# Windowed attention and a feed-forward layer on one core: the order of the instructions set by a list schedule inside the kernel

## The chip, the cores and the metric

One core of a Trainium2 chip runs the kernel alone. The metric is the device time of one execution in microseconds (us), lower is better; a kernel is given by the median of its runs. The core's engines each work through a queue of their own in order: TensorE (PE: matmuls, and PEld: its weight loads), VectorE (DVE), ScalarE (ACT), GpSimd (POOL) and SyncE (SP), whose queue issues the transfers here. An instruction that waits for another engine holds up everything behind it on its own engine.

## The reference

Attention over 8 batches, 8 heads, 576 positions and 64 values a head, with a causal window of 128 and a bias that falls with the distance; its output, as 4608 tokens of 512 values, goes through a feed-forward layer of 2048 hidden units with a piecewise quadratic gate.

```python
scores = scale * np.matmul(q, k.transpose(0, 1, 3, 2))
bias = slopes[:, None, None] * (-np.abs(rel).astype(np.float32))[None, :, :]
mask = (rel >= 0) & (rel < window)
scores = np.where(mask, scores + bias[None], -1000000000.0)
scores = scores - np.max(scores, axis=-1, keepdims=True)
attn = np.exp(scores)
attn = attn / (np.sum(attn, axis=-1, keepdims=True) + 1e-09)
x = np.matmul(attn, v)
...
h = x @ w_in
g = np.where(pos, h, np.where(neg, 0.0, (h + beta) ** 2 / (4.0 * beta)))
return (g @ w_out).astype(np.float32)
```

The inputs q, k and v are float32; the two weight matrices come as 64-bit floats and are turned into 32-bit ones in the kernel.

## The kernel before

The 4608 tokens are cut into ten chunks (`SIZES`): the first and the last have 256 tokens, the eight between them 512. A chunk goes through attention head by head and then through a sweep of the feed-forward layer over eight groups of hidden units. The attention of chunk c+1 is woven into the sweep of chunk c, so that TensorE has both kinds of work.

**Attention of a head m** (steps `scores`, `weights_t`, `values`). TensorE multiplies queries and keys for two blocks of 128 queries at a time into one PSUM bank (`s`); VectorE picks the older or newer key of each place and adds the distance (L304, L306, result `z`, with the maximum `nmax`); ScalarE takes the exponential with the sum (L308); VectorE makes the reciprocal `rc` (L310, L311); the weights are scaled (L316 on ScalarE, four instructions of one block; L313 on VectorE in the first three chunks); TensorE turns them over (`p`, L324); ScalarE and VectorE split them into a rounded high part and a rest (`lu`, L340, L341); GpSimd masks both parts with two instructions over 1024 columns (L348, L350); TensorE multiplies with the values (`x`, L379), and ScalarE and VectorE put the result into `xn` (L384, L385). Before that, ScalarE and VectorE split keys (`kk`, `kl`: L261, L262, one instruction each over both heads of a pair), queries (`ql`: L250, L251) and values (`vs`: L271, L272). In the first three chunks (`LIGHT`) the matmuls are plain float32 ones without a split.

**A sweep** (`sweep_steps`). For each of the eight groups g of a 512-token chunk, seven products after Strassen's scheme (`PRODUCTS`, six matmuls of 256 columns each, L427) replace the eight of the plain one. They use two PSUM banks in turn, `hA` and `hB`. After products 0, 2 and 4 (weights A11, S2, S1) ScalarE copies `hA` out into `s0`, `s2`, `s4` (L561); after product 5 (S4) it copies `hA` into `h0` (L567); VectorE adds `hB` and such a copy after products 1, 4 and 6 (L563, L565, L569). A bank takes its next product only after that. Then the gate (`nonlinear`): clamp on VectorE (L434, `m`), square on ScalarE (L435), maximum on VectorE (L440), rounded copy `gh` on ScalarE (L447), rest `gl` on VectorE (L448). The second layer (`layer2`) then takes three matmuls of 512 columns for each of 16 hidden blocks and four token tiles (L462, L463, L464); each finished tile is copied out as `o` (L467) and stored.

The inputs of a sweep are seven combinations of quarters of `xn`, split again into two parts (`split_x`, `combine`; `x_T1`, `x_B11` and so on). The combinations of weights are made once in the sweep of chunk 1 (`build`), written to device memory, and fetched again for each later chunk (`fetch`, L182) into a ring of ten buffers, one fetch for each product used. All transfers go through the one SP queue.

**What sets the order.** The program is written in the order in which the loops at the end call the steps, and the framework's scheduler then places the instructions of each engine after a model of their times; a few stretches are raised or lowered by hand (`high_priority` with `URGENT` for the copies and adds that free a bank, `issue_after` for the conversion of weights). The framework places single matmuls, so those of a product or of a layer-2 tile can be parted.

Of the kernel before, what the change touches and what calls it, by code (L numbers as in the profile page):

```python
# [8 lines left out]
F32 = mybir.dt.float32  # L9
# [23 lines left out]

@with_exitstack
def windowed_attention_then_ffn(
# [29 lines left out]
    const = ctx.enter_context(tc.tile_pool(name="const", bufs=1))  # L65
    wp = ctx.enter_context(tc.tile_pool(name="wp", bufs=NFC + 1))
    ring = ctx.enter_context(tc.tile_pool(name="ring", bufs=10))
    xp = ctx.enter_context(tc.tile_pool(name="xp", bufs=1))
    fp = ctx.enter_context(tc.tile_pool(name="fp", bufs=2))
    ap = ctx.enter_context(tc.tile_pool(name="ap", bufs=1))  # L70
    dr = ctx.enter_context(tc.tile_pool(name="dr", bufs=1, space=DRAM))
    ps_acc = ctx.enter_context(tc.tile_pool(name="ps_acc", bufs=2, space=PSUM))
    ps_h = ctx.enter_context(tc.tile_pool(name="ps_h", bufs=1, space=PSUM))
    ps_a = ctx.enter_context(tc.tile_pool(name="ps_a", bufs=2, space=PSUM))

    turn = [0]

    def bank(c, name):
        turn[0] += 1
        if c < FIRST and turn[0] % 2:  # L80
            return ps_acc.tile([P, 4 * P], F32, name=name, tag="acc1")
        return ps_a.tile([P, 4 * P], F32, name=name, tag="ps_a")
# [15 lines left out]
    dist = ap.tile([P, P], I32, name="dist", tag="qr")  # L98
# [3 lines left out]
    t = ap.tile([P, 2, P], F32, name="t", tag="kr")  # L102
    V.tensor_copy(t[:, 0], dist)
    V.tensor_scalar(t[:, 1], t[:, 0], float(-P), None, ALU.add)
    V.tensor_scalar(older, t[:, 0], 0.0, None, ALU.is_gt)
    V.copy_predicated(t[:, 0], older, t[:, 1])
    V.tensor_copy(rel[:, 0], t[:, 0])
    G.affine_select(out=rel[:, 1], in_=t[:, 0], pattern=[[-1, P]], base=0, channel_multiplier=1,
                    compare_op=ALU.is_ge, fill=NEG)
    V.tensor_copy(rel[:, 2], t[:, 0])  # L110
    V.tensor_copy(rel[D:, 2], rel[D:, 1])
    V.memset(rel[D:, 2, :D], NEG)
    V.tensor_copy(rel[:, 3], t[:, 0])
# [7 lines left out]
    w_of = {}  # L121
    raw = {}
# [5 lines left out]
    def fetch_raw(i):  # L128
        fc, n = WEIGHTS[i]
        r = raw[i] = xp.tile([P, DM, 2], I32, name=f"raw_{i}", tag=RAW_IN[i % len(RAW_IN)])  # L130
        DMA.dma_start(r.rearrange("p f w -> p (f w)"), (wo32 if n else wi32)[fc])

    def convert(i):
        fc, n = WEIGHTS[i]
        r = raw.pop(i)
        low, high = r[..., 0], r[..., 1]
        if fc not in w_of:
            w_of[fc] = wp.tile([P, 2, DM], F32, name=f"w{fc}", tag="w")
# [575 lines left out]
```

## Time and profile before

| what | us |
|---|---|
| median of 3 runs | 1096.57 |
| lowest and highest of them | 1090.62, 1100.12 |
| the profiled execution | 1102.9 |
| its span, first to last instruction | 1101.2 |

The profile is of one execution. "Busy" of an engine is the time in which at least one of its instructions was running. Matmuls overlap one another, and their ends are modelled, so the rate of TensorE is read from the times between starts. The granted clock of TensorE is given as a share of its full clock. In the answers that list waits, the first name waited for the second; in those that list windows, each engine has its busy time and in brackets how many instructions.

### The profile page before, as it was taken

What the parts mean: (1) busy time and instruction counts of PE and PEld (TensorE: products, weight loads), DVE (VectorE), ACT (ScalarE), POOL (GpSimd) and SP (SyncE); (2) the same over time, 40 slices, a digit from 0 to 9 for tenths busy, and PEclk for the clock granted to TensorE, in tenths of its full rate; (3) what the DMA queues carried; (4) which work ended last, traced back from release to release, by engine and by line L of the source; (5) the groups of instructions that cost most, each with busy time, mean ns of one, the idle gap of its engine ahead of it and who ended that gap; (6) DMA issues with size and microseconds to landing.
All of it is one profiled execution on the core that took longest, in us unless ns stands there. A gap on an engine that the chain in (4) does not pass through costs nothing.

```text
span 1101.2 us, 19641 instructions
## 1 busy us (share of the span) xinstructions
PE 1037.2 (94%) x6432; PEld 914.3 (83%) x6432; DVE 810.6 (74%) x2058; ACT 724.4 (66%) x1850; POOL 202.2 (18%) x226
## 2 busy tenths in 40 slices
PE   7899899998999999998989899989999999999998
PEld 6677688897888788887878788978887888889897
DVE  6888788887667887586768777687758766875453
ACT  6987577666667777566757676667756766764342
POOL 2311333311102021021111211112102111221000
PEclk8999999999999999998999999999989999999999
DMA  9683554556555666556656566565655655665562
GB/s 320 199 280 114 176 177 164 182 186 193 179 170 170 196 189 182 153 162 196 177 147 187 177 185 184 156 207 162 181 155 175 206 156 168 176 204 163 152 220 67
DMA packets 101909, 198.04 MB, mean 180 GB/s; under 512 B 11312, under 2 KB 14896, under 8 KB 101808
## 3 DMA queue, kind: packets, MB, share of 16 engines
q1 hardware_dynamic: 101808, 196.78, 58.3%
q8 instruction: 52, 0.85, 0.3%
q14 instruction: 49, 0.40, 0.1%
HBM read 170.52 MB, written 26.21 MB: 179 GB/s over the span
## 4 chain that ended last, share of the span: by engine, by line
PE 71%; DVE 14%; ACT 8%; issue 4%; DMA 2%; SPq 0%; POOL 0%; DVEq 0%; ACTq 0%; POOLq 0%
PE hA L427 12%; PE acc L462 11%; PE acc L463 10%; PE acc L464 9%; PE hB L427 9%; PE x L379 5%; PE acc L459 2%; PE h L623 2%; PE p L324 2%; PE h L427 2%; PE s L299 2%; PE s L301 2%; DVE ql L251 2%; PE s L302 2%; DVE m L434 2%
## 5 line engine op out<-in xcount | busy, mean ns | idle before, releaser
L462 PE MATMUL acc<-wo,gh 128*128 128x512 f32 x544 | 221.6, 407 | 9.1 <-ACT gh L447 8.6
L463 PE MATMUL acc<-wo,gh 128*128 128x512 f32 x544 | 217.9, 401 | 0.0
L348 POOL TENSOR_SCALAR_AFFINE_SELECT lu<-lu 128x1024 fp32r<-128x1024 f32 (+1 forms) x64 | 69.6, 1088 | 631.1 <-DVE lu L341 572.5
L464 PE MATMUL acc<-wo,gl 128*128 128x512 f32 x544 | 166.9, 396 | 0.3 <-DVE gl L448 0.2
L435 ACT ACTIVATE m<-m,half 128x512 f32<-128x512 f32 (+1 forms) x160 | 107.7, 679 | 65.0 <-DVE m L434 62.5
L308 ACT ACTIVATE z<-z,nmax 128x128 f32<-128x128 f32 x288 | 113.5, 396 | 42.3 <-DVE nmax L306 40.6
L462 PEld LDWEIGHTS acc<-wo,gh 128*128 128x128 f32 x544 | 105.3, 194 | 31.1 <-ACT gh L447 12.3
L463 PEld LDWEIGHTS acc<-wo,gh 128*128 128x128 f32 x544 | 105.2, 193 | 18.4
L434 DVE TENSOR_SCALAR m<-h 128x512 f32<-128x512 f32 (+1 forms) x160 | 78.8, 500 | 55.8 <-ACT h L567 42.4
L427 PE MATMUL hA<-x_T,w_S 128*128 128x256 f32 x672 | 103.8, 289 | 9.7 <-ACT s L561 8.1
L464 PEld LDWEIGHTS acc<-wo,gl 128*128 128x128 f32 x544 | 96.1, 189 | 15.1 <-DVE gl L448 1.0
L427 PEld LDWEIGHTS hA<-x_T,w_S 128*128 128x128 f32 x672 | 92.6, 192 | 18.7 <-ACT s L561 12.0
L561 ACT COPY s<-hA 128x256 f32<-128x256 f32 x192 | 70.3, 366 | 57.5 <-PE hA L427 53.4
L440 DVE TENSOR_TENSOR h<-h,m 128x512 f32<-128x512 f32 x128 | 97.2, 765 | 5.8 <-ACT m L435 5.0
L448 DVE TENSOR_TENSOR gl<-h,gh 128x512 fp32r<-128x512 f32 x128 | 96.8, 765 | 3.5 <-ACT gh L447 2.8
L304 DVE COPY_PREDICATED s<-older,s 128x256 f32<-128x256 uint32 x144 | 60.6, 421 | 43.0 <-PE s L302 33.5
L447 ACT CAST gh<-h 128x512 fp32r<-128x512 f32 x128 | 78.0, 618 | 16.4 <-DVE h L440 16.1
L316 ACT ACTIVATE z<-z,rc 128x128 f32<-128x128 f32 x208 | 67.3, 391 | 24.0 <-DVE rc L311 23.4
L379 PEld LDWEIGHTS x<-lu,vs 128*128 128x128 f32 x528 | 71.5, 190 | 3.5 <-POOL lu L348 0.5
L306 DVE CUSTOM_DVE_ANT_0 z<-s,rel 128x128 f32<-128x128 f32 x288 | 71.7, 284 | 2.3
L379 PE MATMUL x<-lu,vs 128*128 128x256 f32 (+1 forms) x528 | 72.7, 272 | 0.3 <-POOL lu L348 0.3
L350 POOL TENSOR_SCALAR_AFFINE_SELECT lu<-lu 128x1024 fp32r<-128x1024 f32 (+1 forms) x64 | 70.2, 1097 | 6.5 <-DVE lu L341 2.4
(125 smaller groups left out, 2155.3 us busy)
## 6 DMA issues: line engine op xcount, KB each, us to landing
w_S<-d_S SPq DMA_DIRECT2D x224, 256.0 KB, 3.1
w_A<-d_A SPq DMA_DIRECT2D x200, 256.0 KB, 2.8
kr<-in_k_dram SPq DMA_DIRECT2D x57, 320.0 KB, 4.8
vn<-in_v_dram SPq DMA_DIRECT2D x33, 320.0 KB, 3.2
out_dram<-o SPq DMA_DIRECT2D x36, 256.0 KB, 2.5
qr<-in_q_dram SPq DMA_DIRECT2D x33, 256.0 KB, 4.6
raw<-in_moe_w_in_dram SPq DMA_DIRECT2D x16, 512.0 KB, 5.1
raw<-in_moe_w_out_dram SPq DMA_DIRECT2D x16, 512.0 KB, 4.5
```

What stands on the lines that cost most here:

```text
L306: V.tensor_tensor_reduce(out=z[:, i], in0=pt[:, n, P:], in1=distances(b0 + i), op0=ALU.add, op1=ALU.min, scale=-slope, scalar=3.0e38, accu ...
L308: S.activation(z[:, i], z[:, i], AF.Exp, bias=nmax[:, i:i + 1], scale=-1.0, accum_out=sm[:, i:i + 1])
L379: T.matmul(px[:, q0 * P:q1 * P], st, mv.rearrange("p a w -> p (a w)"), start=(w == 0), stop=(w == len(todo) - 1), skip_group_check=True)
L427: T.matmul(o, w[:, a, kb], x[:, b, kb], start=start and n == 0, stop=stop and n == len(todo) - 1, skip_group_check=True)
L434: V.tensor_scalar(m, h, 1.0, -1.0, ALU.min, ALU.max)
L435: a = S.activation(m, m, AF.Square, bias=half[:, 0:1], scale=0.5)
L440: b = V.tensor_tensor(f, h, m, ALU.max)
L447: S.copy(gh, f)
L448: V.tensor_tensor(gl, f, gh.bitcast(F32), ALU.subtract)
L462: T.matmul(a, gh[:, ts], w[:, 0], start=first, stop=False)
L463: T.matmul(a, gh[:, ts], w[:, 1], start=False, stop=False)
L464: T.matmul(a, gl[:, ts], w[:, 0], start=False, stop=last)
```

## The change

The steps no longer issue instructions as they are called. Each step hands a node to a `Plan`: a function that issues it, what it reads and writes, and for each engine that may do it how long it holds the engine and when its result is there. The numbers are fixed in the source, per element and kind. `Plan.deadlines` gives each TensorE node the time at which it would run were TensorE never idle, and every other node the latest time at which its followers are still in time. `Plan.schedule` then plays all engines forward: whenever an engine is free it takes, of the nodes that are ready, the one with the earliest latest time, unless a more urgent one becomes ready soon. `emit` issues everything in the order of the planned starts, with the framework's own placing switched off.

```diff
+class Plan:
+    CROSS, SAME = 0.09, 0.04
...
+    def deadlines(self):
+        t = 0.0
+        for n in self.nodes:
+            if "PE" in n.alts:
+                n.nominal = t
+                t += n.alts["PE"][0]
+        for n in reversed(self.nodes):
+            late = n.nominal if "PE" in n.alts else t + 5.0
+            for s in n.next:
+                late = min(late, s.late - min(a[1] for a in n.alts.values()) - self.CROSS)
+            n.late = late
+            if "PE" in n.alts:
+                n.late = min(n.late, n.nominal)
...
+            cands = [(n.late, n.index, n, r) for n, r in avail[e] if r <= t + 1e-9]
...
+            cands.sort(key=lambda x: x[:2])
...
+    def emit(self, tc, engines, bandwidth):
+        order = self.schedule(engines, bandwidth)
+        with tc.manual_schedule():
+            for n in order:
+                n.alts[n.eng][2]()
+        return order
...
+    def dve(n, f, port=False):
+        return {"DVE": (n * 0.00104 + 0.068, n * 0.00104 + 0.155, f, port)}
...
+    def act(n, f, extra=0.092):
+        return {"ACT": (n * 0.00083 + extra, n * 0.00083 + extra + 0.105, f, False)}
...
+    def pe(t, f):
+        return {"PE": (t, t + 0.2, f, False)}
+
+    def dma(nbytes, f):
+        return {"SP": (0.4, 2.0, f, nbytes)}
+
+    MM = {128: 0.112, 256: 0.118, 512: 0.230}
...
-        S.copy(kk[:, :, :n], kr[:, :, :n])
-        V.tensor_tensor(kl[:, :, :n], kr[:, :, :n], kk[:, :, :n].bitcast(F32), ALU.subtract)
+        for j in range(2):
+            plan.op(act(n, lambda j=j: S.copy(kk.t[:, j, :n], kr()[:, j])), [(b, key)], [(kk, j)])
+            plan.op(dve(n, lambda j=j: V.tensor_tensor(kl.t[:, j, :n], kr()[:, j], kk.t[:, j, :n].bitcast(F32),
+                                                       ALU.subtract), True), [(b, key), (kk, j)], [(kl, j)])
...
+            alts = dve(nb * P, lambda: V.tensor_tensor(
+                z.t[:, :nb], z.t[:, :nb], rc.t[:, :nb].unsqueeze(2).broadcast_to([P, nb, P]), ALU.mult), True)
+            alts["ACT"] = (nb * 0.293, nb * 0.293 + 0.1, by_act, False)
+            plan.op(alts, [z, rc], [z])
...
+            plan.op(pool(nb * P * 0.00114 + 0.07, lambda s=s, mask=mask: mask(s, True)), [(lu, (s, 1))], [(lu, (s, 0))])
+            plan.op(pool(nb * P * 0.00114 + 0.07, lambda s=s, mask=mask: mask(s, False)), [(lu, (s, 1))], [(lu, (s, 1))])
...
+        plan.op(pe(6 * MM[256], f), [w, x], [o])
...
+            plan.op(pe(3 * MM[512], f), [gh, gl, w], [a])
...
+                    plan.op(pe(NCC * 0.43, f), [(w, 0), x], [h])
...
+    plan.emit(tc, ("PE", "ACT", "DVE", "POOL", "SP"), 270e3)
```

Beside the order four things differ. The split of the keys is two instructions on each engine instead of one (24 pairs of heads in the 512-token chunks). The masks of the split weights are four GpSimd instructions of 512 columns instead of two of 1024. The scaling of the weights, the plain copies out of PSUM in the first three chunks, the copies of finished tiles and the sums of weight quarters may go to either of two engines: of the scalings 156 instructions on ScalarE and 39 on VectorE come out, where there were 208 and 24. And a product, a tile of layer 2, or the first layer of chunk 0 is one node, so its matmuls stay together and start when all that they read is there; in the kernel before, the first layer of chunk 0 began with the heads that were done. The buffers are as many as before, each now in a fixed turn.

The numbers of instructions on TensorE are the same. Where they stand is shown at three places. First TensorE where one group of products ends and the next begins, in the sweep of chunk 5: `hB_5_0` is the bank `hB` in group 0 of that chunk, `w_5_0_A22` the weights of product 6, `w_5_1_A12` those of product 1 of the next group. Before:

```order
L379 MATMUL x_49_7347<-lu_49_7255,vs_24_7138 128x128 x2
L427 MATMUL hA_5_0_7124<-x_5_B22_7090,w_5_0_S4_7034 128x256 x6
L427 MATMUL hB_5_0_7125<-x_5_T4_7118,w_5_0_A22_7042 128x256 x6
L427 MATMUL hB_5_1_7361<-x_5_B21_7015,w_5_1_A12_7088 128x256 x6
L427 MATMUL hA_5_1_7360<-x_5_B11_7003,w_5_1_A11_7062 128x256 x6
L324 MATMUL p_50_7418<-ident_84,z_50_7277 128x128
```

The same step one group on, now:

```order
L760 MATMUL acc_5_2_7546<-wo0_514,gl_5_0_7470 128x512
L718 MATMUL hB_5_1_7409<-x_5_T4_7270,w_5_1_A22_7275 128x256 x6
L758 MATMUL acc_5_3_7567<-wo0_514,gh_5_0_7449 128x512
L759 MATMUL acc_5_3_7567<-wo0_514,gh_5_0_7449 128x512
L760 MATMUL acc_5_3_7567<-wo0_514,gl_5_0_7470 128x512
L718 MATMUL hA_5_2_7579<-x_5_B11_7063,w_5_2_A11_7311 128x256 x6
L718 MATMUL hB_5_2_7589<-x_5_B21_7112,w_5_2_A12_7347 128x256 x6
```

Two products into the same bank stood back to back; a tile of layer 2 and a product into the other bank stand between them now.

Second TensorE at the start of group 5 in the sweep of chunk 4, from the product with A11 to the next one into the same bank, with S2. Before:

```order
L302 MATMUL s_47_2_6760<-kl_23_6455,ql_23_6481 128x256
L427 MATMUL hA_4_5_6644<-x_4_B11_5581,w_4_5_A11_6376 128x256 x6
L427 MATMUL hB_4_5_6645<-x_4_B21_5593,w_4_5_A12_6413 128x256 x6
L379 MATMUL x_46_6852<-lu_46_6701,vs_23_6670 128x128 x2
L379 MATMUL x_46_6852<-lu_46_6701,vs_23_6670 128x256 x6
L379 MATMUL x_46_6852<-lu_46_6701,vs_23_6670 128x128 x2
L427 MATMUL hA_4_5_6644<-x_4_T2_5672,w_4_5_S2_6449 128x256 x6
```

Now:

```order
L718 MATMUL hA_4_5_6684<-x_4_B11_5623,w_4_5_A11_6431 128x256 x6
L718 MATMUL hB_4_5_6694<-x_4_B21_5672,w_4_5_A12_6463 128x256 x6
L758 MATMUL acc_4_0_6068<-wo11_2037,gh_4_11_6572 128x512
L759 MATMUL acc_4_0_6068<-wo11_2037,gh_4_11_6572 128x512
L760 MATMUL acc_4_0_6068<-wo11_2037,gl_4_11_6579 128x512
L758 MATMUL acc_4_1_6078<-wo11_2037,gh_4_11_6572 128x512
L759 MATMUL acc_4_1_6078<-wo11_2037,gh_4_11_6572 128x512
L760 MATMUL acc_4_1_6078<-wo11_2037,gl_4_11_6579 128x512
L718 MATMUL hA_4_5_6684<-x_4_T2_5753,w_4_5_S2_6488 128x256 x6
```

Ten matmuls of a head and one product stood between the two, and six matmuls of layer 2 and one product stand there now.

Third ScalarE at that same step, from the copy that ends group 4 (`h0_4_4`) to the one that frees `hA` after the product with A11 (`s0_4_5`). Before:

```order
L567 COPY h0_4_4_6460<-hA_4_4_6458 128x256
L261 CAST kk_24_6799<-kr_24_6488 128x1280
L435 ACTIVATE m_4_4_6582<-m_4_4_6582,half_89 128x512
L250 ACTIVATE ql_24_6826<-qr_24_6486 64x512 x2
L435 ACTIVATE m_4_12_6602<-m_4_12_6602,half_89 128x512
L561 COPY s0_4_5_6654<-hA_4_5_6644 128x256
```

Now:

```order
L862 COPY h0_4_4_6527<-hA_4_4_6491 128x256
L560 ACTIVATE z_46_6634,sum_46_6641<-z_46_6634,nmax_46_6635 128x128 x2
L731 ACTIVATE m_4_4_6649<-m_4_4_6649,half_83 128x512
L740 CAST gh_4_4_6677<-h0_4_4_6527 128x512
L731 ACTIVATE m_4_12_6679<-m_4_12_6679,half_83 128x512
L560 ACTIVATE z_46_6634,sum_46_6641<-z_46_6634,nmax_46_6635 128x128 x2
L856 COPY s0_4_5_6705<-hA_4_5_6684 128x256
```

The split of the next pair's keys and queries has left this stretch, and two pairs of exponentials and a rounded copy `gh` have come into it.

More of the change, by code (lines that the diff above doesn't have):

```diff
@@ L31, with __init__, t @@
 RAW_IN = ("B11", "B21", "T2", "T1", "B22", "T3")
+class Buf:
+    def __init__(self, make, before):
+        self.make, self.before, self.tile = make, before, None
+        self.nodes, self.writers, self.readers = [], {}, {}
+    @property
+    def t(self):
+        if self.tile is None:
+            self.tile = self.make()
+        return self.tile
+class Node:
+    def __init__(self, alts, deps):
+        self.alts, self.deps = alts, deps
+        self.next, self.late, self.start, self.end, self.eng = [], None, None, None, None
@@ L145, in convert @@
-        V.tensor_scalar(o, high, 3, None, ALU.logical_shift_left)
-        if not SIGN_BY_SLOPE:
-            V.scalar_tensor_tensor(o, high, -0x80000000, o, ALU.bitwise_and, ALU.bitwise_or)
-        V.tensor_tensor(o, o, low, ALU.add)
-    def split_out(fc):
-        f = w_of[fc][:, 1]
-        w = w_of[fc] = wp.tile([P, 2, DM], F32R, name=f"wo{fc}", tag="w")
-        S.copy(w[:, 0], f)
-        V.tensor_tensor(w[:, 1], f, w[:, 0].bitcast(F32), ALU.subtract)
-    scratch = {}
-    sums_w = {}
+            w_of[fc] = buf("wp", "w", NFC + 1, [P, 2, DM], F32, f"w{fc}")
@@ L326, in weights_t @@
             if c < FIRST:
-                own, old = [fp.tile([P, 4, P], F32, name=f"{x}_{m}", tag=x, bufs=4)[:, :nb] for x in ("gh", "gl")]
-            else:
-                both = ap.tile([P, 2, 8, P], F32, name=f"lu_{m}", tag="lu")
-                own, old = both[:, 0, :nb], both[:, 1, :nb]
-            head[m]["lu"] = own, old
-            copied = S.copy(own, pt)
-            G.affine_select(out=old, in_=own, pattern=[[0, nb], [-1, P]],
-                            base=0, channel_multiplier=1, compare_op=ALU.is_gt, fill=0.0)
@@ L521, in windowed_attention_then_ffn @@
     have, asked = {}, [0]
+    AHEAD = 10
+    place_w = {key: n for n, key in enumerate(todo_w)}
     def operands_upto(n):
@@ L527, in operands_upto @@
             asked[0] += 1
-    AHEAD = 10
-    URGENT = 200
-    place_w = {key: n for n, key in enumerate(todo_w)}
-    def use(c, g, x):
-        return have[c, g, x]
     def used(c, g, x):
@@ L538, in used, with second @@
         operands_upto(place_w[c, g, x] + 1 + AHEAD)
+    waiting = []
+    def second(keep=4):
+        if len(waiting) > keep:
+            waiting.pop(0)()
     def sweep_steps(c):
@@ L632, in first_sweep @@
         return steps
-    idle = ps_h.tile([P, 4 * P], F32, name="idle", tag="hA")
-    def keep_busy(n):
-        with tc.high_priority(offset=-40):
-            for i in range(n):
-                T.transpose(idle[:, i % 4 * P:(i % 4 + 1) * P], ident, ident)
+    idle = bank("hA", 1, "idle")
+    plan.op(pe(2.0, lambda: [T.transpose(idle.t[:, i % 4 * P:(i % 4 + 1) * P], ident, ident) for i in range(16)]), (), [idle])
     for p in range(NPAIR):
```

673 lines of the change are left out of this document (426 added, 247 removed).

## The prediction

> **What bounds the kernel now.** I read the page's busy times first, then windows cut at the starts of the sweeps, then the waits of TensorE, and last the timeline at two of those waits. The page's first line names the engine:
>
> ```profile
> PE 1037.2 (94%) x6432; PEld 914.3 (83%) x6432; DVE 810.6 (74%) x2058; ACT 724.4 (66%) x1850; POOL 202.2 (18%) x226
> ```
>
> TensorE is the bound, but 94% says little, since matmuls overlap and a matmul that is held counts as busy. What it could do is read from runs of matmuls that nothing holds. These timeline rows give start, length, and how many:
>
> ```profile
> 511.21 0.88 PE L427 MATMUL hA<-x_T,w_S 128*128 128x256 f32 x6
> 510.06 1.09 PE L464 MATMUL acc<-wo,gl 128*128 128x512 f32 x4
> 560.20 1.35 PE L379 MATMUL x<-lu,vs 128*128 128x128 f32 x10
> 558.28 0.28 PE L301 MATMUL s<-kk,ql 128*128 128x256 f32 x1
> 558.40 0.28 PE L302 MATMUL s<-kl,ql 128*128 128x256 f32 x1
> ```
>
> A single 256-column matmul takes 0.28 us and its neighbour starts 0.12 us later, so six take 0.28 + 5 x 0.12 = 0.88: one each 0.12 us. Four of 512 columns take 0.39 + 3 x 0.23: one each 0.23 us. Ten of the values: about 0.11 us each. A sweep over 512 tokens with a full chunk's attention beside it therefore needs 8 x 7 x 6 x 0.12 = 40.3 us of products, 16 x 4 x 3 x 0.23 = 44.2 of layer 2, and for each of 8 heads 8 x 0.12 of scores, 4 x 0.11 of turning and 10 x 0.11 of values, 2.5 us, 19.8 together: 104.3 us. The windows (length, then busy time and count of each engine, then granted clock and transfers), cut where the blocks of 336 products begin; 602.6 to 719.4 is one sweep out of the six from 245 to 950:
>
> ```profile
> 0.00:119.20 119.20, 107.98 (x528) 83.82 (x529) 93.70 (x302) 91.98 (x241) 28.70 (x58) 0.97 0.66 224
> 119.20:245.00 125.80, 120.11 (x766) 107.55 (x765) 105.74 (x276) 85.60 (x236) 35.37 (x42) 0.99 0.53 176
> 245.00:950.00 705.00, 663.32 (x4224) 592.13 (x4223) 528.23 (x1282) 477.72 (x1209) 121.66 (x100) 0.98 0.60 177
> 602.60:719.40 116.80, 109.82 (x707) 97.87 (x706) 89.35 (x214) 79.29 (x201) 20.50 (x16) 0.99 0.61 179
> 950.00:1046.00 96.00, 95.15 (x608) 85.48 (x606) 57.68 (x145) 50.41 (x127) 16.47 (x28) 1.00 0.56 172
> 1046.00:1101.20 55.20, 50.63 (x314) 45.32 (x312) 25.29 (x58) 18.64 (x39) 0.00 (x0) 0.98 0.45 144
> ```
>
> Six sweeps (chunks 2 to 7) need 6 x 104.3 = 625.8 us and take 705: 79 too many. The sweep over chunk 8 shows that this is no fault of the cadence: it has the attention of a half chunk beside it (4 x 0.12 + 2 x 0.11 + 6 x 0.11 a head, 10.9 us), needs 84.5 + 10.9 = 95.4, and takes 96.0. There VectorE is 60% busy; in the six it is 75%, and VectorE and ScalarE are late now and then. The 79 us have three parts: TensorE idle, 705 - 663.3 = 41.7; the clock, 2% of 705 = 14; and 23 that is left, matmuls held so briefly that the modelled ends hide it. Chunk 1 has 5.7 idle and 1.3 of clock.
>
> What the idle time waits for, in the six sweeps (total, times, longest):
>
> ```profile
> PE hB L427 <- DVE h L569: 11.8, 9, 3.2
> PE hA L427 <- ACT s L561: 8.9, 10, 1.4
> PE acc L462 <- ACT gh L447: 6.8, 7, 2.0
> PE p L324 <- ACT z L316: 4.4, 5, 1.1
> PE hB L427 <- DVE h L563: 3.2, 5, 0.8
> PE hA L427 <- ACT h L567: 1.6, 7, 0.3
> ```
>
> Mostly a product waits for its bank, which a short copy or add must empty. Two such waits in the timeline, ScalarE's at the second place shown above and VectorE's at the first:
>
> ```profile
> 558.84 1.26 ACT L261 CAST kk<-kr 128x1280 fp32r<-128x1280 f32 x1 [0.58 <-PE s L301]
> 560.01 0.72 ACT L435 ACTIVATE m<-m,half 128x512 f32<-128x512 f32 x1
> 560.63 1.26 ACT L250 ACTIVATE ql<-qr 64x512 fp32r<-64x512 f32 x2
> 561.92 0.72 ACT L435 ACTIVATE m<-m,half 128x512 f32<-128x512 f32 x1
> 562.55 0.35 ACT L561 COPY s<-hA 128x256 f32<-128x256 f32 x1
> 562.96 0.98 PE L427 MATMUL hA<-x_T,w_S 128*128 128x256 f32 x6 [1.41 <-ACT s L561]
> 618.10 0.69 DVE L467 COPY o<-acc 128x512 f32<-128x512 f32 x1
> 618.82 0.42 DVE L569 TENSOR_TENSOR h<-hB,s 128x256 f32<-128x256 f32 x1
> 619.30 0.98 PE L427 MATMUL hB<-x_B,w_A 128*128 128x256 f32 x6 [1.29 <-DVE h L569]
> ```
>
> A copy of 0.35 us stood behind 3.7 us of work for the next pair of heads, and an add of 0.42 behind the copy of a finished tile; TensorE stood still for 1.4 and 1.3 us.
>
> **The change part by part.** *The order at the banks.* At the first place two products into hB stood back to back, so TensorE had nothing to do while VectorE added (0.42 us plus what is ahead of it). Now three matmuls of layer 2 (0.69) and a product into hA (0.72) lie between: 1.4 us of cover against 0.42. At the second place, from the end of product S4 to the product with S2, TensorE had 0.72 + 2 x 0.23 + 4 x 0.12 + 0.72 + 0.72 + 1.1 = 4.2 us, while ScalarE had to do the copy h0 (0.36), the 3.96 us of rows between, and s0 (0.35): 4.7, later still because the first row waited 0.58. Now between A11 and S2 stand 0.72 + 6 x 0.23 = 2.1 us, and ahead of A11 since S4 another two tiles (1.38), a product (0.72), four scores (0.48) and the values (1.1), 3.7: in all 6.5 with A11 itself, against ScalarE's 0.36 + 4 exponentials of 0.4 + 0.72 + 0.62 + 0.72 + 0.35 = 4.4 us. That is 2 us of slack where 0.5 was lacking. If that cover went (VectorE or ScalarE 2 us late), the same wait would be back. The waits for the bank sum to over half of the idle time, and gh is used later too, since whole tiles of layer 2 now trail the gate. I let the 41.7 us fall to 6, one a sweep for what stays late where a sweep's inputs are made.
>
> *The clock.* Where it is halved, TensorE has stood just before. Two such places, each the stretch before and the one of half clock:
>
> ```profile
> 497.94:501.35 3.41, 1.15 (x9) 1.15 (x10) 2.32 (x6) 0.44 (x3) 0.00 (x0) 1.00 0.68 214
> 501.36:508.18 6.82, 6.04 (x27) 5.57 (x26) 4.13 (x12) 5.46 (x15) 0.00 (x0) 0.50 0.65 196
> 794.90:798.31 3.41, 1.51 (x12) 1.16 (x10) 3.35 (x8) 3.33 (x10) 0.00 (x0) 1.00 0.45 150
> 798.32:805.14 6.82, 6.38 (x20) 5.12 (x21) 3.46 (x8) 2.65 (x7) 0.00 (x0) 0.50 0.82 211
> ```
>
> In 3.41 us TensorE was busy for 1.15 and 1.51, and half clock followed. So a wait is paid twice, and with the waits gone the clock's 14 us should fall to about 2.
>
> The Trainium skill, "TensorE: Matmul & The Clock Gate", section "What's actually happening", says that the gate closes after at least one idle window of about 3.4 us. The windows quoted were a third busy and it closed all the same, so this trace does not agree; by the page's wording nothing in these waits closes the gate.
>
> *What is left, 23 us.* Bounds: all of it goes or none. More distance between steps should remove the brief holds too, but not those inside a run; I take half, 12 left. Six sweeps then cost 625.8 + 6 + 2 + 12 = 646 in place of 705: 59 less. Chunk 1: its idle time falls to 1 and its clock is whole, 6 less.
>
> *The start.* Idle time before 119 us is 11.2. The first layer of chunk 0 must now wait for all eight heads; it began with the first ones. The nearest row is that idle time: gone at best, doubled at worst. In the order the scores of chunk 1 stand among the first-layer products and fill in, so I take no change, and keep -8 and +11 for the range. The last stretch, 4.6 idle, stays.
>
> *More instructions and moved ones.* Rows (a mean in ns behind the busy time):
>
> ```profile
> L348 POOL TENSOR_SCALAR_AFFINE_SELECT lu<-lu 128x1024 fp32r<-128x1024 f32 x48 | 60.2, 1254 | 572.5 <-DVE lu L341 572.5
> L333 POOL TENSOR_SCALAR_AFFINE_SELECT lu<-lu 128x512 f32<-128x512 f32 x8 | 5.4, 675 | 41.5 <-ACT lu L332 41.5
> L313 DVE TENSOR_TENSOR z<-z,rc 128x512 f32<-128x512 f32 x16 | 13.0, 816 | 0.2
> L262 DVE TENSOR_TENSOR kl<-kr,kk 128x1280 fp32r<-128x1280 f32 x24 | 37.7, 1571 | 3.9 <-ACT kk L261 3.9
> L262 DVE TENSOR_TENSOR kl<-kr,kk 128x768 fp32r<-128x768 f32 x4 | 4.2, 1038 | 0.0
> ```
>
> Four masks of 512 instead of two of 1024 cost 4 x 0.675 - 2 x 1.254 = 0.19 us a head on an engine that is 18% busy, and the first two no longer wait for VectorE. The key split: 512 fewer elements save 0.53 us, so an instruction's fixed part is 1.571 - 1280 x 0.00104 = 0.24; 24 more cost VectorE 5.8 us. 15 more scalings, 12.2. Together 18 us over the run, 2 a sweep: VectorE goes from 89 of 117 to 91 of some 108, 84%. I cost this at nothing; the 17 us in which it is still free cover it, and if they fail it is the second rival below.
>
> *The sum.* 59 + 6 = 65 less. The profiled execution took 1102.9 (span 1101.2 and 1.7 around it), so its like would take 1038; it lies 6.3 above the median of the runs shown, 1096.57. Taken off that: **1032 us**.
>
> **The rivals.** *The clock does not follow the waits.* Then the half-clock stretches stay, 14 + 1.3 - 2 = 13 us: 1045. Against it is that each quoted stretch follows idle time. "TensorE: Matmul & The Clock Gate" of the Trainium skill, in the section named above, would have it so.
>
> *VectorE sets the pace.* With it 84% busy in a fixed order, a chain through it is late about half as often as now: 21 of the 42 idle, half the clock and all of the 23 stay. The gain is 21 + 7 + 3 = 31: 1066. For it: the 96-us sweep without loss has VectorE at 60%. Against: both places shown have slack of 1 us and more.
>
> *The waits only move.* Banks, gates and inputs of a sweep are the same chains in the same few buffers; if what is ordered first makes the next late, nothing is gained: 1090 to 1100.
>
> *Slower: the one transfer queue.* The new order puts stores and loads of k, q and v between the fetches of weights. Rows (first in total, times, longest; second KB and us to landing):
>
> ```profile
> SPq L469 <- ACT o L467: 28.2, 10, 18.4
> w_S<-d_S SPq DMA_DIRECT2D x224, 256.0 KB, 3.1
> ```
>
> A store has held the queue 18.4 us once. Ten ring buffers at a product each 108 / 56 = 1.9 us are 19 us of cover, 16 after the landing; a store issued ahead of its tile by more than that starves the products. To end 1% slower, 1108, it would need 76 us, 9.5 in each of eight sweeps, so holds of 25 us in each. No fetch shows in TensorE's waits now.
>
> **How the numbers follow.** My forecast, gains of 35 to 90 us with 1032 in the middle: 0.69. Clock apart from the waits, 1045: 0.08. VectorE, 1066: 0.14. Waits only move: 0.05. Transfer queue: 0.04. About 1% (11 us) is what can be told from no change; faster holds the first three, 0.91, same 0.05, slower 0.04. The low end takes all of the idle time and clock, all but a few us of the 23 and the start's 8: 1096.6 - 42 - 14 - 18 - 7 - 8 = 1008. The high end takes in the VectorE case and the start's 11 on top of it: 1078.
>
> **What would show it right or wrong.** Right: sweeps of 105 to 110 us in the windows, TensorE idle under 2 us in each, few half-clock stretches after the start, waits for L561's and L569's successors near zero, ScalarE and VectorE busy as long as before in a shorter span. Wrong: waits for VectorE's gl, lu or x_T in their place; a wait for a fetched weight; half clock without idle time ahead of it; or a start past 125 us.

## Result and profile after

| kernel | median us | lowest to highest | runs |
|---|---|---|---|
| before, timed beside it | 1097.80 | 1090.62 to 1100.12 | 4 |
| after | 1045.66 | 1043.63 to 1048.91 | 4 |

The ratio is 0.954, with an interval of 0.949 to 0.959: 4.6% faster. The profiled execution took 1047.4 us, its span is 1045.7, so 55.5 less than the span before. The first lines of the page, the second and third of them in 40 slices of the span:

```profile
PE 1011.6 (97%) x6432; PEld 907.1 (87%) x6432; DVE 797.6 (76%) x2102; ACT 710.7 (68%) x1827; POOL 210.0 (20%) x319
...
PE   7999999999999999999999999999999999999666
...
PEclk9899999999999999999999999999999999999878
```

TensorE is busy without a dent from the second slice to the last but three, and then falls to 60% at a lower clock. The windows of the changed kernel, cut where its blocks of 336 products begin (length, then busy time and count of TensorE, its weight loads, VectorE, ScalarE and GpSimd, then the granted clock and the transfers):

```profile
0.00:119.45 119.45, 111.10 (x553) 87.04 (x553) 101.78 (x323) 96.96 (x253) 28.37 (x56) 0.97 0.68 235
119.45:227.01 107.56, 107.56 (x723) 98.93 (x721) 98.90 (x256) 83.33 (x232) 31.84 (x39) 1.00 0.59 195
227.01:855.79 628.78, 628.20 (x4219) 576.39 (x4218) 509.84 (x1308) 457.27 (x1168) 134.75 (x192) 1.00 0.68 197
542.30:647.12 104.82, 104.82 (x708) 96.22 (x706) 85.04 (x219) 77.15 (x198) 22.44 (x32) 1.00 0.70 199
855.79:950.67 94.88, 94.88 (x622) 86.50 (x620) 64.67 (x166) 54.08 (x134) 15.03 (x32) 1.00 0.62 184
950.67:1045.70 95.03, 69.89 (x325) 58.24 (x323) 22.45 (x54) 19.06 (x40) 0.00 (x0) 0.83 0.26 81
```

| stretch | before | after | difference |
|---|---|---|---|
| start | 119.2 | 119.5 | +0.3 |
| sweep of chunk 1 | 125.8 | 107.6 | -18.2 |
| sweeps of chunks 2 to 7 | 705.0 | 628.8 | -76.2 |
| sweep of chunk 8 | 96.0 | 94.9 | -1.1 |
| sweep of chunk 9 | 55.2 | 95.0 | +39.8 |

The cuts stand at products, so a row does not hold quite the same work before and after. By the counts of TensorE's instructions the sweep of chunk 1 has 43 fewer (723 for 766), the start 25 more (553 for 528), the sweep of chunk 8 14 more (622 for 608) and the last sweep 11 more (325 for 314). By the times between their starts in the traces (0.43 us for a plain matmul of 512 columns, 0.22 and 0.11 for plain ones of 256 and 128, 0.23 for a split one of 512, 0.12 for a split one of 256) the 43 are worth about 8 us, the 25 about 4 and the 11 about 3.

So the gain is 95 us, and 40 of it is given back in the last sweep. The six full sweeps are 3 us above what TensorE's cadence needs (628.8 against 625.8), and TensorE idles there for 0.6 us in all. The waits of TensorE in the changed kernel over the whole run, the first four and the last of seven (total, times, longest):

```profile
PE h L718 <- DVE g L734: 21.0, 10, 2.1
PE x L655 <- POOL gh L606: 3.1, 2, 2.2
PE idle L926 <- POOL qscale L287: 1.7, 1, 1.7
PE p L587 <- ACT z L569: 1.4, 1, 1.4
...
PE acc L758 <- DVE o L766: 0.6, 1, 0.6
```

The waits for banks behind the copies and adds of Strassen's products are gone from the list. What its last line tells, 0.6 us behind the copy of a finished tile, is the only wait in the six full sweeps. In the place of the old waits stands one new wait, ten times, and all ten are in the last sweep, where a product `h` is the plain one of a 256-token chunk and `g` is the maximum that empties its bank. One of the ten in the timeline (start, length, engine and line, in brackets how long the engine was idle and for what):

```profile
972.06 0.40 PE L758 MATMUL acc<-wo,gh 128*128 128x512 f32 x1
972.29 0.40 PE L759 MATMUL acc<-wo,gh 128*128 128x512 f32 x1
972.53 0.39 PE L760 MATMUL acc<-wo,gl 128*128 128x512 f32 x1
972.72 0.40 ACT L740 CAST gh<-g 128x256 fp32r<-128x256 f32 x1 [3.40 <-PE acc L759]
...
973.16 0.43 DVE L741 TENSOR_TENSOR gl<-g,gh 128x256 fp32r<-128x256 f32 x1 [3.38 <-ACT gh L740]
973.50 0.42 DVE L728 TENSOR_SCALAR m<-h 128x256 f32<-128x256 f32 x1
973.95 0.51 ACT L731 ACTIVATE m<-m,half 128x256 f32<-128x256 f32 x1 [0.34 <-DVE m L728]
974.50 0.42 DVE L734 TENSOR_TENSOR g<-h,m 128x256 f32<-128x256 f32 x1 [0.58 <-ACT m L731]
974.98 1.37 PE L718 MATMUL h<-x_B,w_A 128*128 128x256 f32 x6 [2.06 <-DVE g L734]
```

The order of the rows tells the story. ScalarE has stood for 3.40 us before the rounded copy `gh`, because the buffer it writes is still read by a matmul of layer 2 (L759). VectorE has stood for 3.38 us before the rest `gl`, which needs that copy. Behind `gl` in VectorE's fixed order is the clamp of the next hidden block, whose bank has long been full; only when clamp, square and maximum are done may the next product have the bank. TensorE, which released the buffer itself, waits 2.06 us for all of that. Then the clock follows. Four windows of 3.4 us from the same place, in the same columns as above:

```profile
971.90:975.31 3.41, 1.35 (x8) 0.88 (x7) 1.19 (x3) 1.40 (x3) 0.00 (x0) 1.00 0.63 234
975.33:978.73 3.40, 3.40 (x16) 3.11 (x15) 0.00 (x0) 0.00 (x0) 0.00 (x0) 0.50 0.41 151
978.74:982.14 3.40, 1.28 (x7) 0.80 (x7) 1.19 (x3) 1.40 (x3) 0.00 (x0) 1.00 0.23 81
982.16:985.56 3.40, 3.40 (x15) 3.11 (x14) 0.00 (x0) 0.00 (x0) 0.00 (x0) 0.50 0.74 230
```

A window with 1.3 us of work is followed by one at half clock, and that one, filled with work, by one at full clock that has the next wait in it. Nine such pairs follow each other. The first of the ten waits lies across two windows, with 1.3 us idle in the second, and no half clock follows it.

The Trainium skill's "TensorE: Matmul & The Clock Gate", section "What's actually happening", gives half clock "after ≥1 idle window (~3.4µs)". The windows quoted here have 1.3 us of work in 3.4 and half clock follows, so the trace does not agree with the word idle; the window's length agrees, since the nine stretches are 3.41 us long and stand 6.83 us apart.

Why did the plan put `gh` there? A step that writes a buffer waits for the readers of the buffer's last owner, and the plan collects those when the step is made (`node.deps.update(b.before.nodes)`). In the last sweep the tiles of layer 2 are called three groups behind the products (a group has two hidden blocks; twelve tiles are waiting, each group calls four and adds four), while `gh` has four buffers, two a group. So the writer is made before the reader of the same buffer, and the plan does not know that it must wait. On the chip the wait is there all the same, as the row of `gh` shows. In the 512-token sweeps layer 2 is close enough behind, and nothing is missing.

### The profile page after: what moved, and what is told of

It is laid out like the page before. It is cut to its first block, busy times and chain, and to the rows that moved or that the text cites. A ratio compares the mean times of both kernels' runs of the same rounds, so it can differ in the third digit from the quotient of the medians.

```text
span 1045.7 us, 19681 instructions
## 1 busy us (share of the span) xinstructions
PE 1011.6 (97%) x6432; PEld 907.1 (87%) x6432; DVE 797.6 (76%) x2102; ACT 710.7 (68%) x1827; POOL 210.0 (20%) x319
## 4 chain that ended last, share of the span: by engine, by line
PE 95%; DVE 2%; ACT 1%; DMA 1%; issue 1%; POOL 0%; ACTq 0%; POOLq 0%
PE hA L718 17%; PE hB L718 13%; PE acc L758 12%; PE acc L759 12%; PE acc L760 12%; PE x L655 9%; PE h L718 3%; PE p L587 3%; PE s L544 3%; PE h L912 3%; PE acc L753 3%; PE s L546 2%; PE s L547 2%; DMA out_dram<-o 1%; ACT m L731 1%
## 5 line engine op out<-in xcount | busy, mean ns | idle before, releaser
L759 PE MATMUL acc<-wo,gh 128*128 128x512 f32 x544 | 217.6, 400 | 0.0
L760 PE MATMUL acc<-wo,gl 128*128 128x512 f32 x544 | 216.0, 397 | 0.0
L618 POOL TENSOR_SCALAR_AFFINE_SELECT lu<-lu 128x512 fp32r<-128x512 f32 (+1 forms) x112 | 79.8, 713 | 578.9 <-ACT lu L611 571.5
L760 PEld LDWEIGHTS acc<-wo,gl 128*128 128x128 f32 x544 | 104.1, 191 | 24.3
L851 DVE TENSOR_TENSOR h<-hB,s 128x256 f32<-128x256 f32 x192 | 80.8, 421 | 46.4 <-PE hB L718 22.5
L759 PEld LDWEIGHTS acc<-wo,gh 128*128 128x128 f32 x544 | 105.2, 193 | 8.4
L741 DVE TENSOR_TENSOR gl<-h,gh 128x512 fp32r<-128x512 f32 x128 | 94.0, 734 | 16.9 <-ACT gh L740 15.4
L718 PE MATMUL hA<-x_T,w_S 128*128 128x256 f32 x672 | 99.2, 283 | 0.0
L734 DVE TENSOR_TENSOR h<-h,m 128x512 f32<-128x512 f32 x128 | 89.3, 698 | 2.3 <-ACT m L731 2.2
L729 DVE TENSOR_SCALAR m<-h 128x512 f32<-128x512 f32 x128 | 55.4, 433 | 29.8 <-ACT h L862 27.4
L862 ACT COPY h<-hA 128x256 f32<-128x256 f32 x64 | 23.9, 373 | 73.8 <-PE hA L718 73.5
L621 POOL TENSOR_SCALAR_AFFINE_SELECT lu<-lu 128x512 fp32r<-128x512 f32 (+1 forms) x112 | 72.6, 671 | 0.0
L655 PEld LDWEIGHTS x<-lu,vs 128*128 128x128 f32 x528 | 67.5, 189 | 1.9
```

What stands on the lines that cost most here:

```text
L618: G.affine_select(out=lu.t[:, s, 0:2 * nb:2], in_=a.bitcast(F32), pattern=[[0, nb], [-1, P]], base=0, channel_multiplier=1, compare_op=ALU ...
L655: T.matmul(px[:, q0 * P:q1 * P], sv, mv.rearrange("p a w -> p (a w)"), start=(w == 0), stop=(w == len(todo) - 1), skip_group_check=True)
L718: T.matmul(o.t[:, :2 * P], w.t[:, a, kb], x.t[:, b, kb], start=start and n == 0, stop=stop and n == len(todo) - 1, skip_group_check=True)
L734: plan.op(dve(n, lambda: V.tensor_tensor(f.t[:, :n], h.t[:, :n], m.t[:, :n], ALU.max), not h_ps), src + [m], dst)
L741: alts = dve(n, lambda: V.tensor_tensor(gl.t[:, :n], f.t[:, :n], gh.t[:, :n].bitcast(F32), ALU.subtract), True)
L759: T.matmul(a.t, gh.t[:, ts], w.t[:, 1], start=False, stop=False)
```

## The experiments

Line numbers of the profiles shift by the lines that an edit adds. Times are medians of four runs, and the kernels of one table were run side by side.

### The last sweep

*More buffers.* Every other group of the last sweep takes its two `gh` and `gl` from buffers of sweep inputs that are free by then, eight in place of four. The order is the same on every engine.

```diff
-        gh = buf("fp", "gh", 4, [P, 4 * P], F32R, f"gh_{c}_{fc}")
-        gl = buf("fp", "gl", 4, [P, 4 * P], F32R, f"gl_{c}_{fc}")
+        if c == NCHUNK - 1 and fc % 2:
+            spare = buf("xp", ("T1", "T2", "T3", "B22")[spares[0] % 4], 1, [P, 2, 2, 2 * P], F32R, f"sp_{c}_{fc}")
+            spares[0] += 1
+            two = [(spare, j, lambda j=j: spare.t[:, j, 0]) for j in range(2)]
```

> Theory: in the last sweep the plan does not know that a rounded copy gh must wait until layer 2 has read the buffer four blocks back, because that reader is made later in the program than the writer; the copies stand too early in the fixed order and hold the clamps behind them. Twice as many buffers for gh and gl there, in the same order on every engine, take the wait away: the ten waits of 2.1 us and the half clock after them (20 us each way, some 37 in all with the small ones) go, 1010 us. Rival: the chain of clamp, square and maximum at the two banks sets the pace of the last sweep whatever the buffers: 1046, the waits as before.

*The plan is told.* A reader that is made after the buffer's next owner makes that owner wait (and the latest times are worked out from the last steps backwards, since the program's order no longer serves).

```diff
+        for b, _ in reads + writes:
+            if b.after is not None:
+                for d in b.after.nodes:
+                    if d not in node.deps and node not in d.deps:
+                        d.deps.add(node)
+                        node.next.append(d)
```

> The plan is told of the missing waits (a reader that is made after the buffer's next owner makes that owner wait). TensorE's order stays the same to the row; only some 14 instructions each of VectorE and ScalarE move in the last sweep. Theory: the clamps go ahead of the copies that are not ready, the ten waits and their half clock go, 1010 to 1014 us. Rival, that TensorE's order (products six blocks ahead of layer 2) is at fault with four buffers: 1040 or more.

*Layer 2 closer.* The last sweep calls it one group of two hidden blocks behind.

```diff
-                    steps += [[second]] * 2
+                    steps += [[lambda: second(0)]] * (6 if g == 0 else 2)
```

> The last sweep calls layer 2 one block behind the products, not three, so every wait is known to the plan; TensorE's order changes in some 30 rows. Theory: the ten waits and their half clock go, 1010 to 1016 us, a few us more than with more buffers if a block's own chain of 2.5 us now shows once or twice. Rival, that the two banks bind: 1046 or more, since a product has less layer 2 beside it.

*The clock alone.* The order as it is, with turns of the identity into an unused bank ahead of the products that wait.

```diff
+            if awake is not None:
+                for i in range(18):
+                    T.transpose(awake.t[:, i % 4 * P:(i % 4 + 1) * P], ident, ident)
```

> The order of the changed kernel, with 18 turns of the identity into a bank that the last sweep does not use (18 x 0.11 = 2.0 us) ahead of each product that waits there. Theory: the waits stay, but TensorE is not idle in them, the clock is not halved and its 20 us go: 1026 us. Rival, that half clock there does not come from idle time: 1046, with the nine stretches still there. If the turns cost time of their own: above 1046.

| kernel | median us | ratio to before | clock |
|---|---|---|---|
| more buffers | 1008.81 | 0.921 (0.916 to 0.926) | 0.997 |
| the plan is told | 1008.87 | 0.921 (0.916 to 0.925) | 0.996 |
| layer 2 closer | 1009.30 | 0.921 (0.917 to 0.925) | 0.994 |
| turns in the waits | 1034.29 | 0.944 (0.940 to 0.948) | 0.997 |

Three different cures give the same time, 37 us less than the change. The first leaves every order alone, the second leaves TensorE's order alone to the row, so the fault was neither TensorE's products running ahead nor the two banks. It was a copy that stood in ScalarE's and VectorE's order ahead of its time. What VectorE issues at that place after the change (its rows there, with the numbers of tiles; `m` is the clamp, `g` the maximum, `gl` the rest, by hidden block; a copy of a finished tile among them is left out):

```
2066 L728 TENSOR_SCALAR m_2_12875<-h_9_2_12844 128x256
2068 L734 TENSOR_TENSOR g_2_12892<-h_9_2_12844,m_2_12875 128x256
2069 L741 TENSOR_TENSOR gl_2_12905<-g_2_12892,gh_2_12903 128x256
2070 L728 TENSOR_SCALAR m_10_12910<-h_9_2_12879 128x256
2071 L734 TENSOR_TENSOR g_10_12929<-h_9_2_12879,m_10_12910 128x256
```

And when the plan knows the wait:

```
2065 L743 TENSOR_SCALAR m_2_12871<-h_9_2_12840 128x256
2067 L749 TENSOR_TENSOR g_2_12888<-h_9_2_12840,m_2_12871 128x256
2068 L743 TENSOR_SCALAR m_10_12902<-h_9_2_12875 128x256
2069 L749 TENSOR_TENSOR g_10_12923<-h_9_2_12875,m_10_12902 128x256
2070 L756 TENSOR_TENSOR gl_9_12933<-g_9_12850,gh_9_12921 128x256
```

`gl_2` stood right behind `g_2`, ahead of the next clamp; now two clamps and two maxima go first, and behind them comes `gl_9`, the rest of the block before; `gl_2` follows later, when its buffer is free. The last sweep of this kernel, beside its six full sweeps:

```profile
226.48:854.41 627.93, 627.93 (x4219) 576.34 (x4218) 509.61 (x1308) 456.66 (x1168) 134.37 (x192) 1.00 0.69 198
...
949.29:1006.80 57.51, 53.34 (x325) 47.43 (x323) 23.11 (x55) 17.34 (x39) 0.00 (x0) 0.99 0.44 134
```

57.5 us in place of 95.0. The turns show how the 37 us divide. TensorE's clock stays whole with them, and the wait is still there:

```profile
988.47 0.41 ACT L743 CAST gh<-g 128x256 fp32r<-128x256 f32 x1 [3.39 <-PE acc L762]
988.50 2.13 PE L719 MATMUL awake<-ident 128*128 128x128 f32 x18
988.90 0.43 DVE L744 TENSOR_TENSOR gl<-g,gh 128x256 fp32r<-128x256 f32 x1 [3.37 <-ACT gh L743]
...
990.78 0.98 PE L721 MATMUL h<-x_B,w_A 128*128 128x256 f32 x6
...
995.98 0.98 PE L721 MATMUL h<-x_B,w_A 128*128 128x256 f32 x6
```

A hidden block now takes 995.98 - 990.78 = 5.2 us, where it needs 12 x 0.12 + 6 x 0.23 = 2.8: eleven blocks at 2.4 too many are 26, and 25.4 is what this kernel takes more than the one whose plan is told. The turns themselves do not set this pace: they end at 990.63 (988.50 + 2.13), VectorE's maximum `g` ends at 990.72, and the product starts at 990.78. Without the turns a block took 6.7 (from the start at 974.98 shown above, the eighth block on starts at 1028.69). Half clock thus cost 11.4 us (1045.7 - 1034.3), not the 20 expected. I had halved the loss by the records of idle time and clock; with the clock whole, the waits alone cost 25. That the half clock in this sweep comes from the idle time is shown by this run, since it went when only the idle time was filled.

### What of the change carries the gain in the full sweeps

The next four start from the plan that knows its waits, 1008.9 us, or take its order away.

*The order alone*: every step on the engine that it had before, keys and masks whole again.

```diff
-            alts["ACT"] = (nb * 0.293, nb * 0.293 + 0.1, by_act, False)
+            if c >= LIGHT:
+                alts = {"ACT": (nb * 0.293, nb * 0.293 + 0.1, by_act, False)}
...
-        for j in range(2):
-            plan.op(act(n, lambda j=j: S.copy(kk.t[:, j, :n], kr()[:, j])), [(b, key)], [(kk, j)])
+        plan.op(act(2 * n, lambda: S.copy(kk.t[:, :, :n], kr())), [(b, key)], [kk])
```

> The plan with all waits known (1008.9 us), but every step on the engine that it had before the change, and keys and masks in whole instructions again: only the order is left of the change. Theory, that the order alone carries the gain: 1009 to 1018 us. Rival, that the free engine and the halved steps carry a good part of it: 1035 or more, with waits for lu, z or kl on TensorE.

*Flat costs*: the plan's durations for VectorE, ScalarE and GpSimd are one number. Three kinds of step do not go through the functions that are edited and keep their own: the addition of the distance (0.215 us), the exponential (0.385) and the scaling on ScalarE (0.293 a block). So the words "every instruction" in the expectation below go too far.

```diff
-        return {"DVE": (n * 0.00104 + 0.068, n * 0.00104 + 0.155, f, port)}
+        return {"DVE": (0.45, 0.55, f, port)}
...
-        return {"ACT": (n * 0.00083 + extra, n * 0.00083 + extra + 0.105, f, False)}
+        return {"ACT": (0.45, 0.55, f, False)}
```

> The plan with all waits known, but every instruction of VectorE, ScalarE and GpSimd is planned at 0.45 us and 0.55 to its result, whatever its length; TensorE's and the transfers' costs as before. Theory, that the durations from a trace are needed, since a key split of 1.26 us in the wrong place holds a bank for longer than the cover of 1.4 us: 1020 to 1050, with waits for the copies and adds at the banks. Rival, that the order by latest times and TensorE's own costs do it and the cover is wide: 1009 to 1015.

*By place*: of the steps that are ready, the first in the program goes first.

```diff
+        t = 0.0
+        for n in self.nodes:
+            if "PE" in n.alts:
+                t = n.nominal
+            n.late = t
```

> The plan with all waits known and the durations as they are, but each engine takes the ready step that comes first in the program, not the one with the earliest latest time. Theory, that the ranking by need is what empties the banks in time: 1050 to 1100, with waits for the copies out of hA and the adds with hB. Rival, that playing the engines forward with true durations is enough, whatever the rank: 1009 to 1020.

*The framework's placing*: the changed kernel's steps, in the program's order, placed by the framework.

```diff
-        with tc.manual_schedule():
-            for n in order:
-                n.alts[n.eng][2]()
+        for n in self.nodes:
+            n.alts[n.eng][2]()
```

> The steps of the changed kernel, each on the engine that its plan chose, but issued in the program's order and placed by the framework's scheduler as in the kernel before (without its raised stretches). Theory, that the gain is the plan's order: 1085 to 1110, the waits at the banks back. Rival, that whole nodes, halved steps and free engines give it under any order: 1060 or less.

| kernel | median us | ratio to before |
|---|---|---|
| the order alone | 1010.66 | 0.922 (0.917 to 0.928) |
| flat costs | 1010.25 | 0.921 (0.915 to 0.928) |
| by place | 1016.69 | 0.928 (0.922 to 0.933) |
| the framework's placing | 1110.21 | 1.014 (1.007 to 1.021) |

The order carries the gain: without the free engines and the halved steps it is all there but 1.8 us (1010.66 against 1008.87, which was timed in another table), and without the order nothing is left. Neither exact durations for most of the helpers' steps nor the rank by need are wanted for it. With flat costs the six full sweeps take 104.4 to 105.7 us each; by place 104.3 to 106.3, and most of its 8 us are lost at the start, where its first 512-token sweep begins at 124.3 in place of 118.9. Both expectations of mine were wrong. The flat number is no wild one, though: 0.45 us lies near the mean of an instruction of VectorE (797.9 us in 2103, so 0.38) and of ScalarE (707.9 in 1826, 0.39) in the run whose plan is told, if not of GpSimd (209.5 in 319, 0.66). In the framework's placing the six full sweeps take 695.8 us, 9 less than before, the start takes 20 more, and the waits at the banks are back (first lines of its waits):

```profile
PE hA L716 <- ACT s L854: 21.4, 21, 2.5
PE p L585 <- DVE z L569: 7.3, 4, 3.6
PE acc L756 <- ACT gh L738: 6.3, 10, 1.2
PE hB L716 <- DVE h L849: 5.1, 9, 1.0
```

*As written*: is it enough not to let anything be moved? Every engine takes its steps in the order in which the program makes them; from the kernel with layer 2 closer.

```diff
-        order.sort(key=lambda n: (n.start, n.end, n.index))
+        order.sort(key=lambda n: n.index)
```

> The steps of the changed kernel, with layer 2 one block behind in the last sweep (1009.3 us with the plan's order), but every engine issues its steps in the order in which the program makes them; only the choice of engine is left of the plan. In the steady sweeps 96 of 100 rows of TensorE stand where they stood. Theory, that the plan's gain is in VectorE's and ScalarE's order, which the program writes head by head (a reciprocal behind its exponentials ahead of an add that frees a bank): 1040 to 1150, with waits at the banks. Rival, that TensorE's order is all of it and any sensible order beside it does: 1009 to 1020.

*TensorE by need*: its steps lose their place in the program, too.

```diff
-            late = n.nominal if "PE" in n.alts else t + 5.0
+            late = t + 5.0
...
-            if "PE" in n.alts:
-                n.late = min(n.late, n.nominal)
```

> The plan, with layer 2 one block behind in the last sweep (1009.3 us), but TensorE's steps too are ranked by the need of what follows them alone, not by their place in the program: all of its rows move, by 34 on the mean in the steady sweeps, and the tiles of layer 2, which nothing waits for, fall behind the products. Theory, that the gain rests on TensorE keeping the program's mix of products, tiles of layer 2 and attention, so that each bank has its cover: 1040 to 1110, the waits at the banks back. Rival, that playing the engines forward finds the cover in any rank: 1009 to 1020.

| kernel | median us | ratio to before |
|---|---|---|
| as written | 1538.12 | 1.400 (1.397 to 1.403) |
| TensorE by need | 1011.96 | 0.921 (0.919 to 0.924) |

As written, the kernel is 40% slower than before, far beyond the 1150 that I expected, and most of TensorE's waits are for a bank, of up to 11 us (the first of its waits; `s` is a bank of attention):

```profile
PE hA L718 <- ACT s L856: 160.3, 53, 7.1
PE hB L718 <- DVE h L851: 92.6, 59, 5.0
PE s L546 <- DVE lu L612: 57.0, 6, 11.2
```

TensorE stands in almost the same order there as in the plan, so it is the order of the engines beside it that must be played forward. GpSimd and the transfers go as written too, but the waits shown are for VectorE and ScalarE, and TensorE waits for no transfer. And with all of TensorE's rows moved the six sweeps stay at 104.0 to 105.2 us each: there is no one good order of TensorE. The third expectation fell with this, that each bank needs the program's own mix as its cover.

*Single matmuls*, by place, since the framework places those. Each matmul of a product and of a tile is a step of its own:

```diff
-        plan.op(pe(6 * MM[256], f), [w, x], [o])
+            t = MM[256]
+            plan.op({"PE": (t, t + 0.2 if n == len(todo) - 1 else t - 0.04, f, False)}, [(w, a), (x, b)], [o])
```

> The plan with all waits known and ranked by place in the program, as in the run that took 1016.7 us, but each matmul of a product and of a layer-2 tile is a step of its own, as the framework places them. Theory, that steps of a whole product keep a bank's cover together and single matmuls use it up too early: 1035 to 1100, the waits at the banks back. Rival, that the size of the steps does not matter: 1012 to 1022.

*TensorE's times halved*, a set of costs not yet touched:

```diff
-        return {"PE": (t, t + 0.2, f, False)}
+        return {"PE": (0.5 * t, 0.5 * t + 0.2, f, False)}
```

> The plan with all waits known, but TensorE's steps are planned at half of their cadence; the other costs and the rank as they are. Theory, that the time between two products is what the plan has to know, since it decides how much cover a bank needs: planned waits that are none on the chip bunch the products, 1025 to 1090. Rival, that any forward play will do, as with the flat costs of the other engines: 1009 to 1015.

| kernel | median us | ratio to before |
|---|---|---|
| single matmuls, by place | 1016.38 | 0.925 (0.921 to 0.930) |
| TensorE's times halved | 1112.65 | 1.013 (1.009 to 1.018) |

The size of the steps is worth nothing (1016.7 with whole ones). TensorE's times are worth all of it: a plan that is right in everything else, but believes TensorE twice as fast, is no better than the kernel before (I had expected 1025 to 1090). Its six full sweeps take 703.0 us. One of its longest waits, in the timeline of the sweep over chunk 3:

```profile
378.24 0.87 PE L733 MATMUL hA<-x_T,w_S 128*128 128x256 f32 x6
...
379.15 0.37 ACT L871 COPY s<-hA 128x256 f32<-128x256 f32 x1 [3.70 <-PE hA L733]
379.42 0.73 ACT L746 ACTIVATE m<-m,half 128x512 f32<-128x512 f32 x1
380.04 0.39 ACT L575 ACTIVATE z<-z,nmax 128x128 f32<-128x128 f32 x1
...
381.71 0.17 DVE L579 TENSOR_SCALAR rc<-sum 128x4 f32<-128x4 f32 x1 [1.72 <-ACT z L575]
381.79 0.69 DVE L749 TENSOR_TENSOR h<-h,m 128x512 f32<-128x512 f32 x1
382.39 0.42 DVE L866 TENSOR_TENSOR h<-hB,s 128x256 f32<-128x256 f32 x1
...
382.86 1.44 PE L733 MATMUL hB<-x_T,w_S 128*128 128x256 f32 x5 [2.58 <-DVE h L866]
```

ScalarE stood for 3.70 us before a copy out of `hA`. Behind that copy waited a square and four exponentials; VectorE stood 1.72 us for the last of these before the first step of a reciprocal (L579), and behind that came a maximum and the add that frees `hB`, for which TensorE waited 2.58. As in the last sweep of the changed kernel, what stands behind a waiting instruction in a fixed order waits with it.

But here the plan is not taken by surprise. The planned times, worked out from the kernel's own `Plan`, have ScalarE idle for 4.9 us before this very copy, and TensorE for 1.6 us before this product. At half times TensorE has 491 us of work in a plan of 864 us, so a wait of TensorE costs this plan nothing and it has no reason to avoid one; in the plan that is told, TensorE has 982 us of work in 998. That this is why the gain is lost is my reading of one place and of these sums, not shown by itself. Nor do the two runs compare errors of one size: TensorE's times are wrong by a factor of two throughout, the flat number keeps the helpers' times near their mean. No run halves the helpers' times. They also have room for an error: VectorE has 19% and ScalarE 26% of a full sweep to spare (85.0 and 77.2 busy of 104.8), TensorE has none.

The framework's placing and the halved times lose about the same hundred us. Whether the framework errs in TensorE's times as well is not shown by any run here; what it reckoned with is in no trace, and that stays open.

## Why the prediction was right and wrong

The forecast was 1032 us, 65 less in the span; it became 1045.7, 55.5 less in the span. It lies in the range and the sign is right, but that it came so near is luck: errors of opposite sign stand behind it. Against the forecast the six sweeps came out 17 us better, chunk 1 12 and chunk 8 1 better, and the last sweep 40 worse. It is chance, too, that the time is the 1045 of the first rival, whose mechanism is not what was found.

- **The idle time of the six sweeps, 41.7, was to fall to 6.** It fell to 0.6. The mechanism was right: the waits at the banks were the order's, and with the order they went. The rows by which I explained it are one order among many, as the run by need shows; halved times for TensorE in the plan undo the gain.
- **The clock, 14 to 2.** It fell to nothing: 1.00 over the six sweeps. The half clock had followed the waits; the run with the turns shows the same in the last sweep. (Of the two windows that I quoted as a third busy, the second was busy for 1.51 of 3.41 us, 44%.)
- **What is left, 23 to 12.** Mis-sized: 2.4 are left (628.8 - 625.8 - 0.6). That they went with the order fits brief holds of the same kind, too short to be seen as idle, but no row shows them singly. The half that I kept had no row for it. Idle, clock and this term make the six sweeps 17 us better than forecast.
- **Chunk 1, 6 less.** It became 18.2 less, but some 8 of that is work that now stands in other stretches (43 matmuls). Of the other 10 I had the 7 of idle time and clock, less 1, and left out about 3 of the same sort as the 23 above.
- **The start, no change.** Right by its length, 119.2 and 119.5. But 25 more matmuls, some 4 us, stand in it, and its idle time fell from 11.2 to 8.4: the new order gained there what I had left at nothing.
- **Chunk 8 as the proof of the cadence.** I had it need 95.4 us and take 96.0. Its window holds 608 of the 624 matmuls that I counted, some 2 us less, so it lost about 2.5 us, not 0.6. Now it holds 622 and takes 94.9.
- **The cost of more instructions, hidden.** Hidden they are, and they are smaller than said: the split keys cost VectorE 43.6 us for 41.9 and the scalings 24.2 for 16.5, so 9.4 more, not 18. Other rows fell, so that the order alone has VectorE busy for 792.5 us and the plan that is told for 797.9.
- **"The last stretch, 4.6 idle, stays."** This is the step that failed. It became 39.8 longer, with 25 us of TensorE idle (95.03 - 69.89) and a clock of 0.83. I took the stretch's idle time of before as a price for a new order, and did not ask whether the plan knows all the waits there. It was to be read in the code: in this sweep a buffer's reader is called after its next writer. With the wait known the stretch is 57.5, 2.3 above before with 3 us more work in it, and the kernel takes 1009, 1 us above the floor of the range.
- **The rivals.** Clock apart from the waits: no half clock is left in the six sweeps. VectorE as the pace: it is busy for 85 of 104.8 us and no wait in the six sweeps is for it beyond 0.6. Transfers: TensorE waits for no fetched weight. "The waits only move" came true in one place, by another way than said there: not the same chains made late, but one wait that the plan was not told of.

## What to carry to other kernels

A list schedule that is issued as a fixed order is as good as its model of waits: before trusting it, compare each wait in the trace with the plan, above all where a buffer's reader is written after its next writer. Get the times of the engine that bounds the kernel right first: here most steps of the other engines could be planned at one flat number near their mean (1010.3 against 1008.9 us), while halving TensorE's times cost the whole gain (1112.7). How much a factor of two in the other engines' times would cost was not tried. And a stretch that is fine before the change is not thereby fine after it: the price of a new order is to be asked stretch by stretch.

## What was not expected of the hardware

Half clock can fall into a rhythm. Here a wait of 2.1 us stood in each hidden block. With the clock whole a block takes 5.2 us; half clock stretched it to 6.7, close to the 6.83 of two windows, and so every second window ran at half clock, nine times from 975 to 1033 us. It cost 11.4 us on top of the waits, and 18 turns of the identity in each wait were enough to keep the clock whole.
